# One K load on nine DMA engines, and seven split dV stores in place of four, in an attention and MLP gradient kernel on one Trainium2 core

## The chip, the core and the metric

The kernel runs on one core of one Trainium2 chip. The metric is the device time of one execution in microseconds (us). The four timed executions of the kernel before took 402.84 to 403.33 us, their median is 402.9. One execution was profiled; that one took 402.91 us, and the span from its first to its last instruction is 401.0 us. DMA engines are the 16 engines that move data between HBM (the large memory) and SBUF (the core's own, of 128 partitions). They are fed by queues: SP and ACT issue to hardware queues, POOL (GpSimd) to a software queue.

## What is computed

The reference is a gated mix of one decode step of attention over a cache and a small MLP, with all its gradients:

```python
x = A_x                                               # 1 x 1 x 640
g = _sigmoid((x * gate_w).sum(-1, keepdims=True))
a = _A_ref(x, A_k_cache, A_v_cache, A_wq, A_wo)       # 32 heads, 4096 keys, 128 a head
b = _B_ref(x, B_w1, B_b1, B_w2)                       # 640 -> 1728 -> 640, mish
return g * a + (1 - g) * b
...
_out, _vjp = jax.vjp(_f, A_x, A_k_cache, A_v_cache, A_wq, A_wo, B_w1, B_b1, B_w2, gate_w)
```

The outputs are the value and the gradients of all these inputs. The large ones are the K and V caches and their gradients: 32 heads of 4096 x 128 in bf16 each, 1 MB a head. So some 64 heads' worth of 1 MB come in and as many go out; the weights and their gradients are some 15 MB each way in addition.

## The kernel before

One head is one period. In SBUF a head of K or V is a tile of 128 partitions by 32 x 128 elements, so a partition's row is 8 KB and lies in one piece in HBM. `period(h)` computes the softmax of head h, its part of the output, dV as an outer product (`dv_half`, twice), the gradient of the scores, and dQ, and transposes K of head h + 1 on TensorE for the next scores; dK of head h is made in the period of head h + 1 (`dk_half`). Steps of the weights, the gate and the MLP are put between by `slot`, which takes them from a list by kind and by what they depend on.

Loads: before each period the main loop calls `load_k(h + 3)` and `load_v(h + 3)` (L764 and L765). Both issue one DMA of 1 MB on SP (L121, L126). There are four K buffers and four V buffers, so a load waits until the head four before has been used. SP takes its instructions in order. It also loads wo and wq (L136, L131), which the loop calls ahead of `load_k` in some periods. At the end SP stores: dV and dK of the last two heads, the gradient of w1, and parts of the gradients of wq and wo (L642, L627, L629, L743, L767, L375, L793).

Stores: dV and dK of heads up to 29 go out on POOL's queue (`ring`, L115), from five buffers that dV and dK share. A dV store is one DMA of 128 rows, except for the heads that L639 picks: those call `spread` (L644), which cuts the 128 rows into two or three DMAs, of 5, 120 and 3 rows, of 14, 105 and 9, or of 8 and 120, in turn by its counter i. `spread` sets the last dimension of a DMA to one row at most; in the built program each of its rows is two half rows of 4 KB.[...] In the kernel before these are heads 5, 12, 19 and 26, with i from 0 to 3.

Each DMA tells its completion through a semaphore. The building layer has eight for SP's and ACT's DMAs and eight for POOL's, gives them out in turn, and lets each DMA wait for the one that had the same semaphore before it.

The lines that matter are L118 to L121 (the K load), L633 to L642 (the dV store and its choice), L644 to L650 (`spread`), and the calls in the main loop, L756 to L783.

Of the kernel before, what the change touches and what calls it, by code (L numbers as in the profile page):

```python
# [16 lines left out]
def kernel(  # L17
# [24 lines left out]
    nc = tc.nc  # L42
    P = 128
    _, H, Sk, Dh = A_k_cache.shape
# [20 lines left out]
    Kv = A_k_cache.rearrange("b h (p j) d -> (b h) p j d", p=P)  # L65
    Vv = A_v_cache.rearrange("b h (p j) d -> (b h) p j d", p=P)
    dKv = out_2.rearrange("b h (p j) d -> (b h) p j d", p=P)
    dVv = out_3.rearrange("b h (p j) d -> (b h) p j d", p=P)
# [44 lines left out]
    kts, vts, wqs, wos = {}, {}, {}, {}  # L113

    def ring(h):  # L115
        return nc.sync if h >= H - 2 else nc.gpsimd

    def load_k(h):  # L118
        if h < H:
            kts[h] = kv_in.tile([P, J, Dh], BF16, name="Kn", tag="Kn", bufs=KB)  # L120
            nc.sync.dma_start(kts[h][:], Kv[h])  # L121

    def load_v(h):
        if h < H:
# [20 lines left out]
    load_wq(0)  # L145
    load_wo(0)
    load_k(0)
    load_v(0)
    load_k(1)
    load_v(1)  # L150
    load_wo(1)
# [4 lines left out]
    nc.sync.dma_start(b1c[:, 0:FM], b1_v)  # L156
    nc.sync.dma_start(b1c[0:FR, FM:FCN], B_b1[FB:F].rearrange("(p c) -> p c", c=1))
    load_k(2)
    load_v(2)
    load_w2(0)  # L160
# [448 lines left out]
    def outer(dst, col, row, half):  # L609
        n = J // 2  # L610
        a, b = half * n, (half + 1) * n
        nc.vector.tensor_tensor(  # L612
            dst[:, a:b, :].rearrange("p j (a b) -> p j a b", b=2),
            col[:, a:b, :].unsqueeze(2).to_broadcast([P, n, Dh // 2, 2]),
            row.rearrange("p (a b) -> p a b", b=2).unsqueeze(1).to_broadcast([P, n, Dh // 2, 2]),
            ALU.mult)
# [16 lines left out]
    def dv_half(h, half):  # L633
        st = sts[h]
        if half == 0:
            st["dV"] = outs.tile([P, J, Dh], BF16, name="dV_sb", tag="dVK")
        outer(st["dV"], st["p"], gps[h // G]["qd"][:, 1, (h % G) * Dh:(h % G + 1) * Dh], half)
        if half == 1:
            if h % 7 == 5 and h < H - 3:  # L639
                spread(h // 7, dVv[h], st["dV"])  # L640
            else:
                ring(h).dma_start(dVv[h], st["dV"][:])  # L642

    def spread(i, dst, t):  # L644
        src = t[:].rearrange("p j d -> p (j d)")
        out = dst.rearrange("p j d -> p (j d)")
        if i % 3 == 0:
            nc.gpsimd.inc_swdge_sem([], [], mode="reset_dge_cursor")
        for a, b in (((120, 125), (0, 120), (125, 128)), ((0, 14), (14, 119), (119, 128)), ((0, 8), (8, 128)))[i % 3]:
            nc.gpsimd.dma_start(out[a:b, :], src[a:b, :], max_dma_last_dim=J * Dh)  # L650

    def period(h):
# [12 lines left out]
        def o_part(a, b):  # L665
            for j in range(a, b):
# [31 lines left out]
        nc.vector.scalar_tensor_tensor(pj[:], in0=DP[:, 0:J], scalar=1.0, in1=e[:], op0=ALU.mult, op1=ALU.mult,  # L698
                                       accum_out=part[:])
        dv_half(h, 0)  # L700
        nc.tensor.transpose(PT, part[:].to_broadcast([P, P]), ident_f[:])  # L701
        if nxt:
# [6 lines left out]
        nc.vector.scalar_tensor_tensor(ds[:], in0=DP[:, 0:J].unsqueeze(2).to_broadcast([P, J, 2]), scalar=dd[:], in1=p_bf[:],  # L709
                                       op0=ALU.subtract, op1=ALU.mult)  # L710
        dv_half(h, 1)
        nc.vector.tensor_scalar(o_all[:, h:h + 1], O[:, 0:1], rz[:], None, ALU.mult)  # L712
        if nxt:
# [148 lines left out]
```

## Time and profile before

| what | value |
|---|---|
| median of four executions | 402.9 us |
| profiled execution | 402.91 us |
| its span | 401.0 us |
| K load of 1 MB on SP, issue to landing, median of 32 | 23.8 us |
| V load of 1 MB on SP, median of 32 | 28.4 us |
| dV store of 1 MB on POOL, median of 26 | 11.5 us |
| the 120-row pieces of three split stores, median | 12.1 us |
| HBM read and written | 82.03 MB each |
| mean granted TensorE clock | 0.918 |

The page is that of one execution. It gives each engine's busy time, the span in 40 slices, the DMA queues (q1 is SP's, q0 POOL's, q10 ACT's, q8 and q14 fetch instructions), the chain of work that ended last, the costliest groups of instructions and the DMA issues. DMA shares are means over the core's 16 DMA engines. A share a little over 1.00 comes from packets that overlap by some nanoseconds. The trace itself keeps each DMA packet with its queue, start, length and size, without the engine that moved it.

### The profile page before, as it was taken

The numbers are of one execution on the slowest core, as the hardware profiler recorded it, in microseconds if no ns is written. First come the engines' busy times: TensorE is split into PE (matmuls) and PEld (weight loads), VectorE is DVE, ScalarE is ACT, GpSimd is POOL, SyncE is SP. The second block draws the span as 40 slices with busy tenths as digits, with TensorE's granted clock in tenths as the row PEclk, the third lists the DMA queues.
The fourth block names the chain that finished last, engine by engine and source line by source line (L and its number), as shares of the span: only waits on it lengthen the run. The fifth ranks groups of instructions, "written<-read, shape, count | busy, mean of one in ns | idle before, by whom it ended". The sixth has DMA issues, their size and how long they took to land.

```text
span 401.0 us, 13611 instructions
## 1 busy us (share of the span) xinstructions
PE 296.4 (74%) x5872; PEld 268.2 (67%) x5872; DVE 303.5 (76%) x791; ACT 177.1 (44%) x411; POOL 47.2 (12%) x94
## 2 busy tenths in 40 slices
PE   0688898778889888578896988719887888988200
PEld 0588787667878777468876878618776777877200
DVE  3338766655899999757688899837999997899850
ACT  1355555334554555325543556505555455544000
POOL 0001101021111111211111113101111121120000
PEclk9999999979998999869998999968999999999555
DMA  7999999999999999999999999999999999999985
GB/s 288 417 416 400 421 422 423 416 421 423 422 425 422 421 426 416 417 426 423 425 419 423 424 425 417 419 424 423 422 425 424 422 421 418 425 418 419 424 370 223
DMA packets 28360, 164.93 MB, mean 411 GB/s; under 512 B 3260, under 2 KB 3964, under 8 KB 12556
## 3 DMA queue, kind: packets, MB, share of 16 engines
q1 hardware_dynamic: 17136, 93.41, 56.4%
q0 software_dynamic: 11104, 70.64, 42.3%
q8 instruction: 46, 0.75, 0.7%
q14 instruction: 14, 0.11, 0.1%
q10 hardware_dynamic: 60, 0.01, 0.0%
HBM read 82.03 MB, written 82.03 MB: 409 GB/s over the span
## 4 chain that ended last, share of the span: by engine, by line
DVE 37%; DMA 32%; PE 19%; ACT 5%; issue 3%; ACTq 0%; SPq 0%
DMA Kn<-in_A_k_cache_dram 31%; DVE dV_sb L612 9%; DVE dK_sb L612 8%; PE tr L587 8%; DVE junk L385 5%; ACT tT L589 4%; PE sA L667 3%; DVE junk L288 3%; PE sA L596 2%; PE sB L720 2%; DVE junk L537 2%; DVE junk L494 1%; DMA vec_rows<-in_gate_w_dram 1%; DVE wo_g L374 1%; DVE dj L707 1%
## 5 line engine op out<-in xcount | busy, mean ns | idle before, releaser
L589 ACT COPY tT<-tr 128x512 f32<-128x512 f32 x256 | 142.3, 588 | 131.2 <-PE tr L587 130.4
L596 PEld LDWEIGHTS <-tT 128*128 128x128 bf16 x2048 | 79.6, 98 | 39.9 <-ACT tT L589 34.4
L587 PE MATMUL tr<-ident_f,Kn 128*128 128x128 f32 x512 | 82.7, 300 | 9.6 <-DMA Kn<-in_A_k_cache_dram 9.6
L612 DVE TENSOR_TENSOR dV_sb<-p_bf,qd 128x2048 bf16<-128x2048 bf16 x64 | 78.0, 1218 | 0.3 <-issue 0.3
L612 DVE TENSOR_TENSOR dK_sb<-ds_bf,qd 128x2048 bf16<-128x2048 bf16 x64 | 77.7, 1216 | 0.0
L587 PE MATMUL tr<-ident_f,Vn 128*128 128x128 f32 x512 | 73.0, 278 | 0.0
L587 PEld LDWEIGHTS tr<-ident_f,Kn 128*128 128x128 f32 x512 | 61.7, 153 | 11.0 <-issue 10.3
L596 PE MATMUL sA<-qd,tT 128*128 128x48 bf16 x1024 | 48.7, 187 | 23.5 <-ACT dq_all L725 12.7
L587 PEld LDWEIGHTS tr<-ident_f,Vn 128*128 128x128 f32 x512 | 56.4, 142 | 0.0
L596 PE MATMUL sB<-qd,tT 128*128 128x48 bf16 x1024 | 46.1, 183 | 0.0
L667 PEld LDWEIGHTS <-Vn 128*128 128x128 bf16 x1024 | 30.2, 96 | 10.4 <-issue 10.4
L667 PE MATMUL sA<-e_bf,Vn 128*128 128x48 bf16 x1024 | 30.7, 183 | 7.6 <-DVE zs L687 6.0
L629 POOL DMA_DIRECT2D out_dram<-dK_sb x30 | 17.3, 575 | 136.2 <-DVE rz L689 83.5
L720 PE MATMUL sB<-ds_bf,Kn 128*128 128x48 bf16 x1024 | 31.1, 183 | 1.4 <-DVE ds_bf L709 1.4
L671 DVE TENSOR_REDUCE m<-sA 128x1 f32<-128x32 f32 x32 | 6.0, 189 | 33.3 <-PE sA L596 26.8
L642 POOL DMA_DIRECT2D out_dram<-dV_sb x26 | 14.1, 544 | 138.4 <-DVE o_all L712 49.7
L720 PEld LDWEIGHTS <-Kn 128*128 128x128 bf16 x1024 | 28.4, 96 | 1.6 <-issue 1.6
L288 DVE SCALAR_TENSOR_TENSOR junk<-wo_g,da_bc 128x640 bf16<-128x640 bf16 x32 | 26.2, 820 | 1.7 <-ACT da_bc L229 1.1
L385 DVE SCALAR_TENSOR_TENSOR junk<-wq_g,dq_bc 128x1024 bf16<-128x1024 bf16 (+1 forms) x25 | 25.1, 1004 | 0.2
L707 DVE TENSOR_SCALAR_CACHE_REDUCE dj<-sB,rz 128x128 f32<-128x128 f32 x32 | 11.1, 346 | 12.1 <-PE sB L701 12.1
L691 ACT ACTIVATE p_bf<-e_bf,rz 128x64 bf16<-128x64 bf16 x32 | 11.1, 348 | 13.6 <-DVE rz L689 10.6
L698 DVE SCALAR_TENSOR_TENSOR pj<-sB,e_bf 128x32 f32<-128x32 f32 x32 | 6.1, 190 | 12.5 <-PE sB L596 12.4
(152 smaller groups left out, 275.8 us busy)
## 6 DMA issues: line engine op xcount, KB each, us to landing
Kn<-in_A_k_cache_dram SPq DMA_DIRECT2D x32, 1024.0 KB, 23.8
Vn<-in_A_v_cache_dram SPq DMA_DIRECT2D x32, 1024.0 KB, 28.4
out_dram<-dK_sb POOLq DMA_DIRECT2D x30, 1024.0 KB, 11.8
out_dram<-dV_sb POOLq DMA_DIRECT2D x26, 1024.0 KB, 11.5
wq_g<-in_A_wq_dram SPq DMA_DIRECT2D x4, 1280.0 KB, 26.2
wo_g<-in_A_wo_dram SPq DMA_DIRECT2D x8, 640.0 KB, 18.7
out_dram<-wo_g POOLq DMA_DIRECT2D x7, 640.0 KB, 11.4
out_dram<-dwq_t SPq DMA_DIRECT2D x4, 896.0 KB, 19.1
```

Source lines behind the costliest of these rows:

```text
L288: nc.vector.scalar_tensor_tensor(junk[:, 0:D], in0=wos[g][:, i, :], scalar=1.0, in1=da_bc[:], op0=ALU.mult, op1=ALU.mult, accum_out=gp["do ...
L385: nc.vector.scalar_tensor_tensor(junk[:, c0:c1], in0=wqs[w][:, rc, c0:c1], scalar=1.0, in1=dq_bc[:, w * WG * Dh + c0:w * WG * Dh + c1], op ...
L587: nc.tensor.transpose(tp[:, t, :], flat[:, k * P:(k + 1) * P], ident_f[:])
L589: nc.scalar.copy(sb[:].rearrange("p a b -> p (a b)"), tp[:].rearrange("p a b -> p (a b)"))
L596: nc.tensor.matmul(out[:, 2 * k:2 * k + W], lhsT=tb[:, t, par, :], rhs=vec[:, par, :].unsqueeze(1).to_broadcast([P, W // 2, 2]), start=(pa ...
L612: nc.vector.tensor_tensor(dst[:, a:b, :].rearrange("p j (a b) -> p j a b", b=2), col[:, a:b, :].unsqueeze(2).to_broadcast([P, n, Dh // 2, 2]),
L629: ring(h).dma_start(dKv[h], st["dK"][:])
L642: ring(h).dma_start(dVv[h], st["dV"][:])
L667: nc.tensor.matmul(O, lhsT=vts[h][:, j, :], rhs=st["e"][:, j:j + 1].to_broadcast([P, W]), start=(j == 0), stop=(j == J - 1))
L691: nc.scalar.activation(p_bf[:], e[:].unsqueeze(2).to_broadcast([P, J, 2]), ACT.Copy, scale=rz[:])
L707: nc.vector.tensor_scalar(dj[:], PT, rz[:], None, ALU.mult, ALU.add, accum_out=dd[:])
L720: nc.tensor.matmul(DQ, lhsT=kts[h][:, j, :], rhs=ds[:, j, 0:1].to_broadcast([P, W]), start=(j == 0), stop=(j == J - 1))
```

## The change

K of head 18 is loaded by five DMAs: four of 27 rows each, taking every fourth row from row 0, 1, 2 and 3 up to row 107, and one of the last 20 rows. All other loads stay. The dV stores of heads 2, 6, 10, 14, 18, 22 and 26 are split, with i from 0 to 6, in place of those of heads 5, 12, 19 and 26 with i from 0 to 3. So there are three more split stores, one more of each of the three kinds[...]. The bytes moved are the same. `spread` is not changed. In the built program POOL has six more instructions, SP four more DMAs, and the order on TensorE, VectorE and ScalarE is as before.

```diff
@@ -118,7 +118,12 @@
     def load_k(h):
         if h < H:
             kts[h] = kv_in.tile([P, J, Dh], BF16, name="Kn", tag="Kn", bufs=KB)
-            nc.sync.dma_start(kts[h][:], Kv[h])
+            if h == 18:
+                for c in range(4):
+                    nc.sync.dma_start(kts[h][c:108:4], Kv[h][c:108:4])
+                nc.sync.dma_start(kts[h][108:P], Kv[h][108:P])
+            else:
+                nc.sync.dma_start(kts[h][:], Kv[h])
 
     def load_v(h):
         if h < H:
@@ -636,8 +641,8 @@
             st["dV"] = outs.tile([P, J, Dh], BF16, name="dV_sb", tag="dVK")
         outer(st["dV"], st["p"], gps[h // G]["qd"][:, 1, (h % G) * Dh:(h % G + 1) * Dh], half)
         if half == 1:
-            if h % 7 == 5 and h < H - 3:
-                spread(h // 7, dVv[h], st["dV"])
+            if h % 4 == 2 and h < H - 3:
+                spread(h // 4, dVv[h], st["dV"])
             else:
                 ring(h).dma_start(dVv[h], st["dV"][:])
 
```

## The prediction

> **What bounds the kernel now.** I read the page's header and its parts 2 and 3 first, then the chain (part 4), then the busy time by stretches at the end, then SP's own waits, and last the DMA packets of the trace one by one.
>
> ```profile
> span 401.0 us, 13611 instructions
> PE 296.4 (74%) x5872; PEld 268.2 (67%) x5872; DVE 303.5 (76%) x791; ACT 177.1 (44%) x411; POOL 47.2 (12%) x94
> DMA  7999999999999999999999999999999999999985
> DMA packets 28360, 164.93 MB, mean 411 GB/s; under 512 B 3260, under 2 KB 3964, under 8 KB 12556
> q1 hardware_dynamic: 17136, 93.41, 56.4%
> q0 software_dynamic: 11104, 70.64, 42.3%
> q8 instruction: 46, 0.75, 0.7%
> q14 instruction: 14, 0.11, 0.1%
> ```
>
> No compute engine is over 76%; the DMA engines are at nine tenths or more in 37 of 40 slices. Part 4 puts "DMA Kn<-in_A_k_cache_dram 31%" on the chain: compute waits for K. So the end is set by when the DMA engines are through, and the question is whether all 16 are through together:
>
> ```profile
> 386.00:388.00 2.00, 0.36 (x2) 0.50 0.84 349
> 388.00:390.00 2.00, 0.00 (x0) 0.50 0.69 289
> ...
> 395.00:396.00 1.00, 0.00 (x0) 0.50 0.69 271
> 396.00:397.00 1.00, 0.00 (x0) 0.50 0.58 221
> 397.00:398.00 1.00, 0.00 (x0) 0.50 0.45 163
> 398.00:399.00 1.00, 0.00 (x0) 0.50 0.20 70
> 399.00:400.00 1.00, 0.00 (x0) 0.50 0.04 13
> ```
>
> (stretch; its length; DVE busy; PE clock; DMA share; GB/s). They are not. From 388 to 390 the share is 0.69, eleven engines of 16; from 398 on three, then one. No instruction is issued after SP's last store at 392.23: these last microseconds are backlog of the engines that are behind.
>
> The trace gives no packet's engine, but a packet on a busy engine starts 3 or 4 ns before the one before it ends, and each engine takes its rows of each DMA in the order of issue. Linked by that, the 28,360 packets make 16 chains (two that run in step can be confused for a while). Ends of their last packets: five are through with all that was issued by 386.5 to 387.4, a sixth at 389.8 (these wait for SP's last two stores); one ends at 396.4; eight at 396.8, 397.1, 397.9, 397.9, 398.4, 398.4, 398.4, 398.7; the last, X, at 399.6, and the span ends 1.4 later. From 17 us on those last ten hardly have a gap, so **the time is the sum of work on the fullest engine**. Why they differ: the eight share the 46 instruction packets of q8 (about 1.0 us each, five or six a chain, in a fixed turn), the early ones have none. X's packets are stretched (mostly 313 to 326 ns for 8 KB instead of 309), some 15 us in all. The four split stores of the kernel before relieve X: in them the others moved 16 or 18 half rows, X 4, 4, 2 and 4.
>
> [...]
>
> From the odd rows of the four stores the chains' places follow: 0 to 3 are two early chains, the one of 389.8 and the one of 396.4; 5 and 6 are the two of 397.9, both of the loaded eight; 7 to 12 are two early ones and four of the eight (396.8, 397.1, 398.4, 398.4); 13 to 15 one early and two of the eight (398.4, 398.7).
>
> **The change part by part.** A row is 8 KB: 309 ns less 3 of overlap, 306. A half row of a split store is 159, about 155 net, so 311 a row.
>
> Three more split dV stores (heads 2, 6, 10, 14, 18, 22, 26 in place of 5, 12, 19, 26). Of the stores' three kinds, one more of each. X: 24 rows (7.34 us) become 5 (1.55) and some 60 four-byte packets of 6 ns net (0.36): -5.4 us. Every other engine: 24 rows become 25 (+0.31; 26 on engines 0 to 3, +0.62), and each store costs 8 x 5 ns for half rows and two more completions, 0.05, so +0.16: +0.47, or +0.78. POOL issues six more instructions, about 0.6 us each by "81.90 1.92 ... x3"; POOL is 12% busy and waits for DVE, so nothing.
>
> K of head 18. Engines 0 to 8: 8 rows become 4 x 3 + 2 = 14, +1.84, and four completions, 0.02: +1.86. Engine 9: 2 rows, -1.8. Engines 10 to 15: none, -2.45.
>
> Sums: X 399.6 - 5.4 + 1.9 = 396.1. Engines 5 and 6: 397.9 + 2.33 = 400.3. Engines 7 and 8: the turn of q8 goes ..., 398.7, 398.4, the two of 397.9, 398.4, 398.4, 397.1, 396.8; if it rises with the number, 7 and 8 are the two of 398.4: 400.7. The one of 396.4 (0 to 3): 399.0. Engines 9 to 15: all earlier by 1.4 to 2.0. So the fullest engine ends 0.7 to 1.1 later than X did; I take 400.7, **+1.1 us**. The relief of X is real but others stood only 0.9 behind it, and K of head 18 is put on some of those.
>
> SP's queue. K of head 18 is issued as five DMAs. In the built program SP's DMAs take eight completion semaphores in turn, and each waits for the one eight before. Before shows such a wait, on a store that needs nothing of what it waits for:
>
> ```profile
> SPq L121 <- PE sB L720: 160.6, 18, 17.6
> SPq L375 <- DMA out_dram<-dV_sb: 9.5, 1, 9.5
> ```
>
> So the third to fifth piece and V of head 18 wait for earlier loads:
>
> ```profile
> 179.07 0.33 SPq L121 DMA_DIRECT2D Kn<-in_A_k_cache_dram  x1
> 179.45 0.48 SPq L126 DMA_DIRECT2D Vn<-in_A_v_cache_dram  x1
> 188.41 0.33 SPq L136 DMA_DIRECT2D wo_g<-in_A_wo_dram  x1
> 188.86 0.40 SPq L121 DMA_DIRECT2D Kn<-in_A_k_cache_dram  x1
> 189.30 0.46 SPq L126 DMA_DIRECT2D Vn<-in_A_v_cache_dram  x1
> ```
>
> K of head 17 (issued 179.07) landed at 204.2, so V of head 18 goes out at about 204 instead of 189.3; the next K behind it at 209 (197.7), its V at 214.6. Behind SP stands nothing but loads. At 204 a loaded engine still has V of head 17, wo and its rows of K to move, until 211 to 217; I cost it at nothing for them. The early engines run dry of loads for some us and have 9 to spare. If the cover fails, each us of gap on a full engine is a us at the end: 0 to +2.[...] The wait of PE for K of head 18 is set by engines 5 to 8, about 217 + 1.9, near X's 219 before: no change.
>
> Profiled execution: 402.91, its span 401.0; the median of the four is 402.9, so no correction. 402.9 + 1.1 = **404.0**.
>
> **Rivals.** (A) the forecast, 403.4 to 404.8: 0.50. (B) the nine engines hold fewer of the loaded ones than I place there, or engines 7 and 8 are early ones. With one loaded engine among them the end is between the 399.0 of the 396.4 chain and 400.7: 402.3 to 403.7, about 403.1. For it: loading nine unloaded engines would make sense[...]. 0.27. (C) SP's waits starve full engines[...]: one to three us more, 404.8 to 406.5. For it: SP loses 15 us of lead; against: the backlog above. 0.13. (D) the other side: X alone sets the end, on the runs without profile more than here, and the relief counts in full until the next loaded engine, 398.7 - 2.0, or the 399.0 chain: at most -0.9, 402.0; it decides only if no loaded engine is in 0 to 8 and X costs more than I read. 0.10[...].
>
> **How the numbers follow.** This kernel's measurement can tell about 0.2%, 0.8 us: faster is under 402.1, slower over 403.7. A lies for the greater part above 403.7, C wholly, B mostly within, D under or near 402.1. Faster 0.09, same 0.31, slower 0.60. The range 402.3 to 405.3 leaves out the far ends of C and D.
>
> **What would show it.** The DMA share of the last stretches: 0.04 at 399 to 400 rising to two or four engines' worth (0.12 to 0.25) there and falling to nothing by 401. V of head 18 issued near 204 with SP waiting for a load. X no longer last. Wrong if the share at the end falls earlier than before, if K of head 18 lands after 222, or if DMA shows slices under nine between 190 and 230.

## The result, and the profile after

| | before | after |
|---|---|---|
| median of the timed executions | 402.75 us (64 executions) | 404.59 us (43 executions) |
| profiled execution | 402.91 us | 403.87 us |
| its span | 401.0 us | 402.1 us |

The ratio is 1.0041, with a 95% interval of 1.0034 to 1.0049: the change costs 0.0041 x 402.75 = 1.65 us (1.4 to 2.0). The two profiled executions differ by 1.0. The changed kernel has two groups of executions: five took 402.65 to 402.95 us, the time of before, and 31 of the others 404.1 to 405.1. The profiled one lies between them. The ratio compares means of executions, with three slow ones of 408.7 us and more left out.

The page of the changed kernel, its header and its parts 2 and 3:

```profile
span 402.1 us, 13628 instructions
PE 298.3 (74%) x5872; PEld 270.3 (67%) x5872; DVE 303.2 (75%) x791; ACT 177.5 (44%) x411; POOL 50.9 (13%) x99
DMA  8999999999999999999999999999999999999995
DMA packets 28982, 164.93 MB, mean 410 GB/s; under 512 B 3498, under 2 KB 4202, under 8 KB 13562
q1 hardware_dynamic: 17166, 93.41, 56.4%
q0 software_dynamic: 11696, 70.64, 42.5%
```

The DMA engines are as full as before, with the same bytes. q1 has 30 packets more: K of head 18 now ends with 4 x 9 + 10 = 46 completions of four bytes in place of 16, so its pieces were on nine and ten engines, as foretold, if each engine sends one completion, as the 16 of a plain load suggest. The busy time by stretches at the end (stretch; length; DVE busy; PE clock; DMA share; GB/s):

```profile
388.00:390.00 2.00, 1.86 (x7) 0.50 0.99 413
...
396.00:397.00 1.00, 0.00 (x0) 0.50 0.64 240
397.00:398.00 1.00, 0.00 (x0) 0.50 0.42 153
398.00:399.00 1.00, 0.00 (x0) 0.50 0.17 64
399.00:400.00 1.00, 0.00 (x0) 0.50 0.08 29
400.00:401.00 1.00, 0.00 (x0) 0.50 0.02 8
```

The last engine works until 400.4, 0.8 us longer than X did before. At 388 to 390, where five engines were idle before (share 0.69), all are at work (0.99). SP's timeline (start; duration; line; output and input; count):

```profile
191.86 4.64 SPq L123 DMA_DIRECT2D Kn<-in_A_k_cache_dram  x4
198.22 0.34 SPq L124 DMA_DIRECT2D Kn<-in_A_k_cache_dram  x1
203.04 0.36 SPq L131 DMA_DIRECT2D Vn<-in_A_v_cache_dram  x1
207.18 0.33 SPq L126 DMA_DIRECT2D Kn<-in_A_k_cache_dram  x1
211.33 0.33 SPq L131 DMA_DIRECT2D Vn<-in_A_v_cache_dram  x1
```

SP waits as foretold: V of head 18 goes out at 203.0, the next K at 207.2, its V at 211.3.

Linked into 16 chains as in the prediction, the packets give the end of each engine. "Early" engines have no instruction packets and end with SP's last stores, after some idle time. The columns of one part alone are the first two experiments below; the last two are a second and a third profile of the changed kernel, executions of 402.80 and 404.32 us. The trace has the ends of the 16 chains. The engines' numbers, here and in the prediction, are the author's estimate, from the half rows that the chains moved in the split stores (X 4, 4, 2 and 4 before, the others 16 or 18); no run shows an engine's number.

| engines | before | predicted | split stores alone | K alone | after, second | after, third |
|---|---|---|---|---|---|---|
| X (4) | 399.6 | 396.1 | 394.4 | 401.2 | 395.9 | 396.7 |
| 5, 6 | 397.9, 397.9 | 400.3 | 397.1, 397.1 | 399.8, 399.8 | 398.8, 399.3 | 399.2, 400.8 |
| instruction packets on 5, 6 | 6, 6 | 6, 6 | 5, 5 | 6, 6 | 5, 5 | 5, 5 |
| 7, 8 | early | 400.7 | early | early | early | early |
| the late one of 0 to 3 | 396.4 | 399.0 | 396.3 | 397.7 | 398.3 | 398.7 |
| the six others of the loaded eight (9 to 15) | 396.8 to 398.7 | 1.4 to 2.0 earlier | 398.4 to 398.8 | 396.6 to 396.8 | 396.3 to 397.5 | 397.0 to 399.3 |

In the third profile X and an early engine can't be told apart in part of the span, so its 396.7 may be 396.6. "After, second" gains 0.3 us on the engines (399.3 against 399.6); "after, third" loses 1.2. What differs between them can be put in one number. Packets of one size mostly take the same time (8 KB on SP's queue: within 2 ns of 309 for 90% of them, before and in the first profile of after); what a packet takes beyond it, summed over all engines from 20 us on, I call the stretch. It was 52 us before (16 of it on X), 72 in the first profile of after, 57 in the second and 78 in the third. 78 less 57 is 21 us, 1.3 us an engine; the two executions differ by 1.5. These bursts can be read in the busy time by stretches, here of the second profile:

```profile
203.00:206.00 3.00, 2.54 (x7) 1.00 1.02 410
206.00:210.00 4.00, 3.93 (x10) 1.00 1.02 418
...
244.00:246.00 2.00, 1.57 (x9) 1.00 1.03 421
246.00:248.00 2.00, 1.96 (x5) 1.00 1.01 393
248.00:250.00 2.00, 0.89 (x4) 1.00 1.05 409
...
340.00:344.00 4.00, 2.95 (x11) 1.00 1.00 418
```

and of the third:

```profile
203.00:206.00 3.00, 2.90 (x7) 1.00 1.03 381
206.00:210.00 4.00, 3.93 (x10) 1.00 1.01 410
...
244.00:246.00 2.00, 1.87 (x8) 1.00 1.06 388
246.00:248.00 2.00, 2.00 (x3) 1.00 1.00 359
248.00:250.00 2.00, 1.57 (x9) 1.00 0.99 373
...
340.00:344.00 4.00, 2.90 (x7) 1.00 1.04 405
```

The share is about 1.00 in both, so the engines look equally busy; only the last column falls. A full share with fewer bytes is what stretched packets look like. (The view counts a packet whole in the stretch in which it starts, so in a burst the share can pass 1.00 by more than the overlap of the packets.)

Where the bursts lie matters for their cause. From 190 to 225 us, when K of head 18 is issued and moved, the stretch is above that of before by about 5 us in the first profile, 5 in the second and 7 in the third. In the second that is all. The other 15 and 19 us or so of the first and third lie at 140 to 160, before K of head 18 is issued, at 225 to 260 and at 330 to 360.

### The profile page after: what moved, and what is told of

The parts are those of the page before. It is cut to its first block, busy times and chain, and to the rows that moved or that the text cites. A ratio compares the mean times of both kernels' runs of the same rounds, so it can differ in the third digit from the quotient of the medians.

```text
span 402.1 us, 13628 instructions
## 1 busy us (share of the span) xinstructions
PE 298.3 (74%) x5872; PEld 270.3 (67%) x5872; DVE 303.2 (75%) x791; ACT 177.5 (44%) x411; POOL 50.9 (13%) x99
## 4 chain that ended last, share of the span: by engine, by line
DVE 40%; DMA 29%; PE 20%; ACT 5%; issue 3%; ACTq 0%
DMA Kn<-in_A_k_cache_dram 20%; DVE dK_sb L617 10%; DVE dV_sb L617 9%; PE tr L592 8%; DMA w2c<-in_B_w_dram 7%; DVE junk L390 4%; ACT tT L594 4%; PE sA L672 3%; DVE junk L293 3%; PE sA L601 3%; PE sB L725 2%; DVE junk L542 2%; DVE junk L499 1%; DMA vec_rows<-in_gate_w_dram 1%; DVE wo_g L379 1%
## 5 line engine op out<-in xcount | busy, mean ns | idle before, releaser
L592 PE MATMUL tr<-ident_f,Vn 128*128 128x128 f32 x512 | 74.5, 282 | 0.0
L592 PEld LDWEIGHTS tr<-ident_f,Vn 128*128 128x128 f32 x512 | 57.5, 144 | 0.0
L647 POOL DMA_DIRECT2D out_dram<-dV_sb x23 | 12.7, 551 | 123.9 <-DVE dV_sb L617 58.0
L655 POOL DMA_DIRECT2D out_dram<-dV_sb x19 | 12.1, 642 | 28.1 <-DVE m L320 28.1
```

The lines of the kernel that those rows point to most:

```text
L592: nc.tensor.transpose(tp[:, t, :], flat[:, k * P:(k + 1) * P], ident_f[:])
```

## The experiments

**One part at a time.** The first two kernels hold one part of the change each; the edits are to the changed kernel.

```diff
-            if h % 4 == 2 and h < H - 3:
-                spread(h // 4, dVv[h], st["dV"])
+            if h % 7 == 5 and h < H - 3:
+                spread(h // 7, dVv[h], st["dV"])
```

> The kernel before with K of head 18 on nine engines alone, its four split stores as they were. Theory 1 (the fullest engine sets the end): X is one of the nine and keeps its stretched packets, 399.6 + 1.86 = 401.5, so +1.9 us (+0.4 to +2.2), more than the changed kernel's. Theory 2 (SP's waits behind the pieces delay the loads and so the end): +1.6 us, as the changed kernel, with or without the split stores. If the three split stores cost the time: within 0.5 us of before.

Measured: 404.94 us against 402.69, ratio 1.0060 (1.0039 to 1.0081), +2.4 us (1.6 to 3.3). The end of the profiled execution:

```profile
398.00:399.00 1.00, 0.00 (x0) 0.50 0.19 71
399.00:400.00 1.00, 0.00 (x0) 0.50 0.17 60
400.00:401.00 1.00, 0.00 (x0) 0.50 0.07 25
```

From 398 to 400 three engines are at work: X and the two of 5 and 6. Then X is alone, to 401.2 where 401.5 was expected; 5 and 6 end at 399.8 as 397.9 + 1.86 says. The time alone can't tell the two theories apart (+1.9 and +1.6 both lie in the interval); these ends can. SP waits here as in the changed kernel (V of head 18 goes out at 204.5, the next K at 209.4), and yet the stretch is 53 us, as before. In this profile the nine engines carry K of head 18 at the price of its rows.

```diff
-            if h == 18:
-                for c in range(4):
...
-            else:
-                nc.sync.dma_start(kts[h][:], Kv[h])
+            nc.sync.dma_start(kts[h][:], Kv[h])
```

> The kernel before with the seven split stores alone, K of head 18 as it was. Theory 1: X is relieved to 394.2, the next engines gain 0.47 and stand at 399.2, 0.4 us before X's old end: -0.4 us (-0.8 to +0.4); the DMA share from 399 to 400 falls to 0.02 or less. Theory 2: no change beyond 0.3 us, for SP is untouched. If the split stores themselves are dearer than 0.47 us an engine: +0.5 to +1.7 us.

Measured: 402.23 us against 402.69, ratio 0.9990 (0.9979 to 1.0000), -0.4 us (-0.8 to 0).

```profile
397.00:398.00 1.00, 0.00 (x0) 0.50 0.42 147
398.00:399.00 1.00, 0.00 (x0) 0.50 0.25 89
399.00:400.00 1.00, 0.00 (x0) 0.50 0.00 0
```

X is out of the way at 394.4 and six loaded engines end together at 398.4 to 398.8. The stretch is 54 us. So in these profiles neither part alone brings much stretch; both together had 57 to 78. The split stores are a small gain by themselves, and not what costs the time.

**Five pieces over all engines.** An edit to the kernel before: K of head 18 in as many DMAs as in the changed one, but meant to be shared alike by all engines.

```diff
+            if h == 18:
+                for a, b in ((0, 32), (32, 64), (64, 96), (96, 112), (112, P)):
+                    nc.sync.dma_start(kts[h][a:b], Kv[h][a:b])
```

> The kernel before with K of head 18 in five DMAs, but of 32, 32, 32, 16 and 16 rows, which all 16 engines share alike: SP's four more turns alone. Theory 1: no engine gets more work than four completions, +0.02 us; no change (-0.4 to +0.4 us), though V of head 18 goes out at 203 to 206 as in the changed kernel. Theory 2: +1 to +2 us.

Measured: 403.45 us against 402.69, ratio 1.0018 (1.0008 to 1.0028), +0.7 us (0.3 to 1.1), though by the author's estimate no engine has more rows. So, if the estimate holds, there is a cost besides the rows, between the two theories. In its profile all 16 engines have stretched packets from 214 to 218, 4.9 us in sum, 0.3 an engine. The last engine, X, ends at 399.9, 0.3 later than before; what the rest of the 0.7 is stays open.

**Rows that lie together.** The changed kernel with other sets of rows.

```diff
-                    nc.sync.dma_start(kts[h][c:108:4], Kv[h][c:108:4])
+                    nc.sync.dma_start(kts[h][27 * c:27 * c + 27], Kv[h][27 * c:27 * c + 27])
```

> The changed kernel with the four sets of 27 rows each in one piece (0 to 26, 27 to 53 and so on) in place of every fourth row. Theory 1: the same as the changed kernel, +1.6 us against before (+1.0 to +2.2). If strided rows collide[...] and that costs the time: at least 0.8 us less than the changed kernel, +0.8 or under.

Measured: 405.55 us against 402.69, ratio 1.0056 (1.0035 to 1.0078), +2.3 us (1.4 to 3.1). Strided rows (+1.65 us) are no disadvantage against rows that lie together; whether either costs more than the usual rows, this doesn't tell. The stretch is 79 us, 20 of it from 200 to 210.

**The changed kernel again, the pieces four times, and another division.** The second profile has the changed kernel's code.

> The changed kernel once more, for a second profile: of its 43 executions five took 402.65 to 402.95 us and most of the others about 404.5, and the profiled one, with 403.87, belongs to neither group. Theory 1 (the fullest engine): in an execution of about 404.5 us the engines that end last are 5 and 6[...] at about 401, and what they carry more than in the first profile can be named (a sixth instruction packet is 1.0 us). Rival: another engine, or all nine engines alike, end last, after a stall between 190 and 230 us.

It took 402.80 us, like the five short executions, and is the column "after, second" of the table. So it can't test the theory for an execution of 404.5. With few bursts its engines end a little earlier than before.

```diff
-            if h == 18:
+            if h in (14, 18, 22, 26):
```

> The kernel before with K of heads 14, 18, 22 and 26, in place of 18 alone, in five DMAs of 32, 32, 32, 16 and 16 rows over all 16 engines. If each such head costs the 0.7 us that one seemed to cost[...]: +2.1 to +3.5 us. If the 0.7 us came from where this one head fell, or from the program's layout: +0.3 to +1.2 us. Theory 1 in its plain form: +0.1 us.

(The edit is to the kernel with five DMAs over all engines.) Measured: 406.65 us against 402.93, ratio 1.0090 (1.0074 to 1.0106), +3.6 us (3.0 to 4.3): 0.9 us a head. In the profiled execution, the longest of the five (407.53 us), the stretch is 110 us, 58 more than before or 3.6 us an engine. After the pieces of head 14, issued at 146.58:

```profile
166.00:168.00 2.00, 1.95 (x8) 1.00 1.00 409
168.00:170.00 2.00, 1.03 (x1) 0.77 1.04 335
170.00:172.00 2.00, 0.52 (x3) 0.50 1.14 320
172.00:174.00 2.00, 2.00 (x5) 0.50 0.96 283
174.00:176.00 2.00, 1.93 (x8) 0.50 0.99 410
```

For six microseconds the engines are full at three quarters of their rate, loads and stores alike.

```diff
-                for c in range(4):
-                    nc.sync.dma_start(kts[h][c:108:4], Kv[h][c:108:4])
-                nc.sync.dma_start(kts[h][108:P], Kv[h][108:P])
+                for a, b in ((0, 25), (25, 121), (121, P)):
+                    nc.sync.dma_start(kts[h][a:b], Kv[h][a:b])
```

> The seven split stores, and K of head 18 in three DMAs of 25 rows[...], 96[...] and 7[...]. Theory 1: the loaded ones of 9 to 15 stood at 398.8 with the seven split stores alone and lose 0.61, engines 5 and 6 lose 0.3, X stands at 394.4 + 1.2 and the fullest of 0 to 3 at 396.3 + 1.2: the end is about 0.6 us before that of the seven stores alone, -1.0 us against before (-1.3 to -0.6). If every K load in pieces costs 0.7 us whatever the engines: +0.1 us (-0.3 to +0.5).

Measured: 403.00 us against 402.93, ratio 1.0009 (1.0000 to 1.0017), +0.4 us (0 to 0.7). This was meant to beat both kernels, and the rival was right. The -1.0 us was the author's estimate from a division of the rows among the engines that no figure of this run shows; the stretch was 73 us, 21 above before or 1.3 an engine, enough to eat the 1.0 us. Here it all lies between 190 and 225. The three DMAs came with bursts, as the changed kernel's five did (57 to 78 us).

**Is it where the rows lie?** K of heads 14, 18, 22 and 26 in eight DMAs of 16 rows: every eighth row in both memories, every eighth in SBUF only, or every eighth in HBM only (three edits to the kernel before, shown in turn). The trace keeps no addresses, so no run shows which rows an engine has in a plain load.

```diff
+                for c in range(8):
+                    nc.sync.dma_start(kts[h][c:P:8], Kv[h][c:P:8])
...
+                    nc.sync.dma_start(kts[h][c:P:8], Kv[h][16 * c:16 * c + 16])
...
+                    nc.sync.dma_start(kts[h][16 * c:16 * c + 16], Kv[h][c:P:8])
```

> K of heads 14, 18, 22 and 26 in eight DMAs of 16 rows each, every eighth row, so that each engine has one row a DMA[...]. Every engine's work is as before but for seven completions a head (0.17 us in all). If SP's turns or the mere number of DMAs cost the 3.6 us of the four heads in five pieces: +3.6 us or more, for SP has more turns here. If the place of the rows costs it ([...]stretched packets on all engines, 110 us summed over them with the five pieces and 52 before): +0.2 us (-0.3 to +0.6), and a stretch of about 52 us.

> As the kernel with eight DMAs of every eighth row, but the rows read from HBM are sixteen that lie together: [...]the engines read neighbouring rows of HBM. (Keys of these four heads come in another order for K than for V, so what is computed differs.) If the writes to SBUF make the stretch: as k_own_four, +0.2 us. If the reads from HBM make it: +2.5 us or more, stretch over 90 us.

> The other way round: every eighth row of HBM[...], written to sixteen partitions that lie together[...]. (The order of keys differs again.) If the writes to SBUF make the stretch: +2.5 us or more, stretch over 90 us. If the reads from HBM make it: +0.2 us.

Measured against 402.89 us, in this order: 405.11, ratio 1.0047 (1.0030 to 1.0064), +1.9 us (1.2 to 2.6); 405.30, 1.0055 (1.0040 to 1.0070), +2.2 (1.6 to 2.8); 405.55, 1.0059 (1.0044 to 1.0074), +2.4 (1.8 to 3.0). The stretch is 110, 96 and 109 us. The first kernel came out as neither of its expectations (+0.2, or +3.6 or more). The intervals overlap: between these three places of the rows no difference can be seen. Eight pieces cost less than five did (+3.6), with as much stretch, so neither the number of pieces nor the stretch alone sets the price. What the three have in common is SP, and the number of pieces and completions. In the first of them the eight pieces of head 22 take SP 29.94 us (237.78 to 267.7), and the engines run dry:

```profile
266.00:267.00 1.00, 0.00 (x0) 0.50 0.86 348
267.00:268.00 1.00, 0.00 (x0) 0.50 0.67 279
268.00:269.00 1.00, 0.16 (x1) 0.50 0.76 295
269.00:270.00 1.00, 0.96 (x4) 0.50 1.10 262
270.00:271.00 1.00, 1.00 (x4) 0.50 1.11 254
```

First the share falls below one, which is starving; then it is full at 60% of the rate, which is stretch, while a row and a completion follow each other on every engine. These kernels don't keep the two apart, and as it is not shown which rows an engine has in a plain load, they can't rule out the place of the rows.

**A third profile, and the split stores one head earlier.**

> The changed kernel a third time, for a profile of an execution near 404.5 us. If the stretched packets make the difference between the executions of about 402.8 and those of about 404.5: a stretch of 75 us or more summed over the engines where the second profile (402.8) has 57, in bursts between 140 and 250 us and after the split stores. If a sixth instruction packet on engines 5 and 6 makes it: a stretch under 60 us and the end at about 401.2 all the same.

It took 404.32 us with a stretch of 78, as the first theory said, and the same five instruction packets on 5 and 6. It is the last column of the table.

```diff
-            if h % 4 == 2 and h < H - 3:
+            if h % 4 == 1 and h < H - 3:
```

> The changed kernel with the seven split stores at heads 1, 5, 9 and so on to 25 in place of 2, 6, 10 to 26: the same number of each kind, but each goes out one head earlier and so no longer right ahead of the loads of wo and wq, which the loop issues at heads 3, 7, 11 and so on. Engine sums are as in the changed kernel without stretched packets, whose second profile took 402.80: about -0.1 us against before. If the bursts of stretched packets in the changed kernel (after its split stores, at 150, 244 to 248 and 342 us) come from the stores meeting these loads: -0.4 to +0.4 us, stretch under 62 us. If they come from nine engines being out of step with the rest, or from split stores wherever they stand: +1.2 to +2.0 us, stretch of 70 us or more.

Measured: 403.98 us against 402.75, ratio 1.0023 (1.0012 to 1.0034), +0.9 us (0.5 to 1.4). That is between the two expectations: about half of the loss goes with the place of the split stores. Both groups are still there: three of the 14 took 402.4 to 403.0 us, most others about 404. The profiled execution (403.22) has a stretch of 65 us, with the bursts moved (150 to 154, 212 to 216). So where the split stores fall matters; that it is their meeting with the loads of wo and wq is not shown, for a store one head earlier meets other traffic too.

## Why the prediction came out

The size was about right, +1.1 forecast and +1.65 measured, but by luck: the engines named for the end were not there, and a cost priced at nothing made up for them. By its steps:

- **The fullest engine sets the end.** Right. Each part alone moved the end as its engine sums say: -0.4 forecast and measured for the split stores, +1.9 and +2.4 for K, with 401.5 and 401.2 for X.
- **X is relieved to 396.1.** Right: 395.9 in the second profile.
- **Engines 5 and 6 at 400.3.** (The sum is 400.2.) They do end last, at 398.8 and 399.3 in the profile with few bursts. The term that was off is the instruction packets: five each instead of six, as in the kernel of split stores alone, so 1.0 us less: 397.9 + 2.33 - 1.0 = 399.2. Which engines get five differs between these programs.
- **Engines 7 and 8 at 400.7.** This is the step that failed: "if it rises with the number, 7 and 8 are the two of 398.4". They are early ones, in every profile in which nine engines could be told from the rest. With K alone only X and the two of 5 and 6 end after 397.7, where two more at 398.4 + 1.86 = 400.3 were implied. Rival B had this. So the six other loaded engines are all among 9 to 15, which the change relieves. The rows and packets of the change then put the last engine at 399.2 or 399.3 against 399.6 before, about -0.3 us, not +1.1.
- **SP's queue at nothing.** The issue times were right within 1.0 us for V of head 18, 1.8 for the next K and 3.3 for its V, and the last rows of K of head 18 were in by 221 (TensorE's wait for them ends at 220.9, 217.1 and 220.2 in the three profiles). The cost was not nothing. "I cost it at nothing" stands against +0.7 us for five pieces over all engines, and 5 to 7 us of extra stretch from 190 to 225, 0.3 to 0.5 an engine, in the changed kernel. That is only a part of the extra stretch, which is (72 - 52) / 16 = 1.3 and (78 - 52) / 16 = 1.6 us an engine in the first and third profiles. The prediction has no term for the rest, which comes elsewhere and in part before K of head 18 is issued. Rival C, one to three us more, expected full engines to starve; what came were bursts of slow packets, stores too, with the DMA slices still at nine. The view that was to show it, "DMA slices under nine between 190 and 230", can't show it, for the share counts a slow packet as busy. The line of GB/s does.
- **The DMA share from 399 to 400 at 0.12 to 0.25.** It was 0.08: one engine in place of two to four, since 7 and 8 were not there.

So the time is that of rival B's engines with stretch on top, about a quarter of it where rival C looked, and by chance the sum lies near the forecast. What is shown: the price of each part alone, that K in pieces over all engines costs by itself, that it grows with the number of such heads, and that the execution of the changed kernel with more stretch took longer by about the stretch of one engine. What stays open is what makes a packet slow in a burst, and so most of the cost. SP's waits alone are not enough, for with K alone they are there and the stretch is not (53 us against 52). The place of the rows stays possible. A load in pieces that costs SP no turn was not tried.

## What to carry to other kernels

When the DMA engines are the bound, add up the work engine by engine, and count the instruction packets too: relief of the slowest engine is worth no more than the distance to the next one after the change, here 0.4 us of 5.4. Before rows are moved from one set of engines to another, find out from a profile of a one-part change which engines the set holds; the place inferred for two engines turned a small gain into a forecast loss. A load cut into pieces can cost more than its packets: over all engines 0.5 to 0.9 us for each such load here, on nine engines alone nothing that could be told from its rows. Look for slow packets in GB/s, not in the DMA share, and see where they lie before you lay them to the change.

## What had not been expected of the hardware

**Two groups of executions, and the granted clock.** In the second profile (402.80 us) and the first (403.87) the compute engines are within 0.4 us of each other until head 6. Then the busy time by stretches (PE busy; PE clock) shows, for the second:

```profile
86.00:88.00 2.00, 2.00 (x37) 0.50 1.02 430
88.00:90.00 2.00, 1.59 (x29) 0.66 1.00 422
90.00:91.00 1.00, 1.00 (x11) 1.00 1.03 434
```

and for the first:

```profile
86.00:88.00 2.00, 2.00 (x38) 0.50 1.02 430
88.00:90.00 2.00, 1.59 (x28) 0.50 0.99 418
90.00:91.00 1.00, 1.00 (x8) 0.50 1.07 451
```

TensorE gets half its clock until 94 in the first and in the third, until 89 in the second. From head 7 to head 13 the first and third run 1.8 to 2.0 us behind the second, so the split store of head 10 goes out at 143.0 and 142.9 in them and at 141.1 in the second. They have a burst at 150 that the second doesn't have. The four other profiles with seven split stores agree: with the stores one head earlier the half clock lasts until 94 and there is a burst at 150; with the split stores alone, the rows together and the three DMAs the clock is full from 88 and there is none. But two of these, the rows together and the three DMAs, have 79 and 73 us of stretch all the same, most of it from 190 to 225. And over all executions of the changed kernel the mean clock is 0.917 to 0.933 in the five short ones and 0.904 to 0.923 in the 31 about 404.6, so they overlap. This is a coincidence in time and not a cause. It may be a part of why one program has two times: the clock moves the stores and loads against each other, and so could decide which of them meet.

**The turn of the instruction packets.** (Places on engines are those of the linked chains.) There are 46 in every profile, on eight engines, so six engines get six and two get five. Which two differs between programs: 5 and 6 had six each in the kernel before and with K alone, and five each with seven split stores. One such packet is 1.0 us on its engine (0.97 in the median before, 1.00 after), more than half of what the whole change cost.
